# A fused scan, MLP and token-mix kernel: the front's steps in a written list, TensorE in the weight conversions, and token-mix weights moved beside the middle MLP blocks

## The chip, the cores and the metric

One core of a Trainium2 chip runs the whole program. The metric is the device time of one execution in microseconds (us); of a kernel the median of its runs is given. The engines in the rows are PE (TensorE; PEld is its weight load), DVE (VectorE), ACT (ScalarE), POOL (GpSimd) and SP, whose queue starts nearly all DMA transfers.

## The reference, cut to what matters

Three parts follow each other. All inputs are 4 batches of 768 positions.

```python
for t in range(768):                                   # attention: 4 x 8 heads, state 48 x 48
    y[:, :, t] = einsum('bhd,bhde->bhe', q_t, state)
    v_old = einsum('bhde,bhd->bhe', state, k_t)        # k normalised by its length
    state += beta_t * outer(k_t, v_t - v_old)
x = y as (4, 768, 384)
u = x + real(fft(fft(x, axis=1), axis=2))              # MLP part
x = u + relu(layernorm(u) @ w_ch1) @ w_ch2             # 384 -> 1536 -> 384
theta = x @ w_theta                                    # token mix
u = x + w_tok_r @ (x * cos(theta)) + w_tok_i @ (x * sin(theta))
out = u + relu(u @ w_ch)
```

The weights come as 64-bit floats, everything else and the output as 32-bit.

## The kernel before, in words

**Precision and conversions.** A product of two fp32 values is made of three passes in the format fp32r, high by high, high by low and low by high (`mm3`, L71 to L74). So each weight is kept as two fp32r tiles, hi and lo. `Split.steps` (L93 to L123) makes them: one step takes a 128 x 384 piece of 64-bit numbers, loads it with a DMA on SP into a raw tile (L107), takes the absolute value of the high words on ScalarE (L110), puts a 32-bit number together with six VectorE instructions (L111 to L116), and makes hi and lo with three GpSimd ones (L120 to L122). w1 and w2 have 12 such pieces each, 24 conversions in all, that take turns three by three. Their tiles are those of the MLP's residual u (two buffers, the raw tile) and of its transposed input uh, ul (one buffer each, the working tiles named w_...ag).

**Attention.** The sequential recurrence is done in chunks of 64 positions. `gram(w)` (L201) loads keys and queries with two DMAs for each half of a step d and makes their products sm on TensorE; `solve(w)` (L223) turns a triangular system for 32 chunk pairs at once by elimination on VectorE, a loop of 30 steps with one product tmp and one sum T each (L258, L261); there are six solves. `load(d)` brings queries, keys and values; `chunks(d)` prepares the scan (the YU tiles take four copies on VectorE, L309 and L315); `scan(g)` carries the state X over one chunk of all heads: short matmuls pu, ps and py (through the helper at L199), with copies and products of X on ScalarE and GpSimd in between. 24 steps d hold 48 scans, 12 to a batch.

**MLP.** After the twelve scans of a batch its Fourier matmuls follow, then three blocks of 256 positions, twelve in all. `prepare`, `prepare_1` (pm, L530) and `prepare_2` make a block's input; then twelve times an up group ph (`ffn_up`, nine matmuls L72 to L74) and a down group pc (`ffn_down`, six matmuls L595 to L598). Block q + 1 is prepared inside block q, at the places f = 0, 4 and 11 (LEAD). A block's result is stored to the scratch x2scr.

**Token mix.** `TokenMix.weights` converts w_theta and w_tok_r beside the last MLP blocks; `late_weights` converts w_tok_i (12 steps) and w_ch (3) once the MLP's w1 and w2 are used up, and into their tiles. `phases(b)` makes for six tiles of 128 positions theta (pth), its sine and cosine (L846 begins the reduction n) and the products z as hi and lo tiles (L862). `run` then makes for each half hf of the positions the sums over w_tok_r (`real`) and w_tok_i (`imaginary`), in PSUM tiles ty, and the last product with w_ch (`channels`). z tiles lie in a pool of their own for the first six and in w2's tiles for three more. Batch 0 has an order of its own, with the real sums of half 0 and two of half 1 ahead of the late conversions.

**What sets the order.** `attention_steps` is a generator; tables say at which d a solve or a gram is issued (SOLVES, GRAMS, AHEAD). `attend(n)` takes n of its pieces between the groups of the MLP; in the front, each piece is followed by one conversion until the first batch has its twelve scans; then nine conversions more (CONV_PRE), then three for each f of the first block as long as any are left. A scheduler (TCARGS) finally orders each engine's instructions by a simulated timeline, so what stands behind what on an engine is to be seen in the order below.

```python
    while not state["fed"]:
        attend(1)
        if state["chunks"] >= CONV_AT:
            late = late or fr.solve_end
            with tc.issue_after(late.ins):
                next(split, None)
```

Of the kernel before, what the change touches and what calls it, by code (L numbers as in the profile page):

```python
# [33 lines left out]
F64_LEAST = 2.0 ** -15  # L34
F64_MOST = float(np.array([0x47EFFE00], np.uint32).view(np.float32)[0])
# [6 lines left out]
SOLVES = (2, 6, 7, 13, 15)  # L42
GRAMS = (1, 6, 9, 13)
CONV_AT = 0
CONV_PRE = 9
# [3 lines left out]
RPACE = 15  # L49
# [3 lines left out]
AHEAD = {3: (), 4: (5,), 5: (6, 7)}  # L53
FIXD = ()
SUBD = 0
# [21 lines left out]
class Split:  # L77
# [15 lines left out]
    def steps(self, stage, act=False):  # L93

        nc, step = self.nc, self.STEP
        for c, s in self.todo:
# [40 lines left out]
class Front:  # L137
# [19 lines left out]
    def open_attention(self, ctx):  # L157
# [43 lines left out]
    def gram(self, w, c0=0, c1=2 * C):  # L201

        nc, FE, TK, B2 = self.nc, self.FE, self.TK, self.B2
        if c0 == 0:
            self.KQ[w] = self.sol.tile([P, NI, 2 * C], F32, tag="KQ", name=f"KQ{w}", bufs=2)
# [3 lines left out]
        for d in range(4 * w, 4 * w + 4):  # L209
            for h in range(0, 8, step):  # L210
                n = slice(8 * (d % 4) + h, 8 * (d % 4) + h + step)
                kt = self.sol.tile([P, step, 8 * C // step], F32, tag="kt", name=f"kt{d}_{h}_{c0}", bufs=NKT)
                for par in range(2):
                    nc.sync.dma_start(kt[FE[par]], src[par, d, :, h:h + step])
                sm = self.mw([P, step, c1 - c0], f"sm{d}_{h}_{c0}")
                for i in range(step):
                    for par in range(2):
                        k = kt[FE[par], i, :]
                        self.mm(sm[TK[par], i, :], k[:, 0:C], k[:, c0:c1])
                nc.scalar.activation(kq[:, n, c0:c1], sm, AF.Copy)  # L220
                if c0 == 0:
                    for par in range(2):
                        (nc.vector if w in FIXD else nc.gpsimd).tensor_copy(kq[B2[par], n, 0:32], kq[B2[par], n, 32:64])  # L223

    def solve(self, w):
        nc, sol, sml = self.nc, self.sol, self.sml
        T = sol.tile([P, 32, 32], F32, tag="T", name=f"T{w}")
        nc.vector.transpose(T.rearrange("p j i -> p j i"), self.KQ[w][:, :, 0:32].rearrange("p n j -> p j n"))
        diag = T.rearrange("p i j -> p (i j)")[:, 0:1024:33]

        def small(nm, bufs=1):
            return sml.tile([P, 32], F32, tag=nm, name=f"{nm}_{w}", bufs=bufs)
# [54 lines left out]
    def chunks(self, d):  # L287
# [3 lines left out]
        if d % 4 == 0:  # L291
            self.solved(d // 4)
# [736 lines left out]
```

## Time and profile before

| | before |
|---|---|
| three runs | 1001.2, 1001.59, 1005.55 us; median 1001.59 |
| profiled execution | span 1217.0 us, 23437 instructions |
| PE | 1126.0 us busy, 93%, 9312 matmuls (PEld 957.3, 79%) |
| DVE | 682.7 us, 56%, 1574 instructions |
| ACT | 394.8 us, 32%, 982 |
| POOL | 387.5 us, 32%, 504 |
| granted TensorE clock, mean | 0.666 of full speed |
| HBM | 58 GB/s over the span |

The profiled execution is the one that all rows come from, and its span is its own time: 215 us more than the median of the runs without a profile. Busy time is what an engine spent in instructions. The page's slices show two parts: in the first eight of 40 (some 240 us) PE is busy 45 to 76% and DVE mostly over 90%; in all others PE is at 90% or more.

### The profile page before, as it was taken

To read this page: it belongs to the slowest core of one execution; us is meant where nothing else is said; L and a number is where in the kernel's file an instruction comes from. 1 tells how busy PE (TensorE), PEld (TensorE's weight loads), DVE (VectorE), ACT (ScalarE), POOL (GpSimd) and SP (SyncE) were. 2 spreads that over 40 slices of the span, in tenths; PEclk is the share of its full clock that TensorE was granted. 3 is DMA by queue.
4 is the path that set the end of the run, shared out by engine and by line. 5 is a ranking of instruction groups with operands and counts; after the bars stand their busy time and mean duration, and the time that the engine had idled before them with its cause. 6 is when DMAs were issued, how large, how long until landed. Compare 5 with 4: busy or idle time off the path is not lost.

```text
span 1217.0 us, 23437 instructions
## 1 busy us (share of the span) xinstructions
PE 1126.0 (93%) x9312; PEld 957.3 (79%) x9312; DVE 682.7 (56%) x1574; ACT 394.8 (32%) x982; POOL 387.5 (32%) x504
## 2 busy tenths in 40 slices
PE   5675664999999999999999999999999999999998
PEld 4564553778788888788888898888988888888887
DVE  5999999645666632576212464744579732450401
ACT  2243343423332343244352121212545411460300
POOL 5257764341131113024120242430235421350210
PEclk9995555666666666666666666666666666666666
DMA  6223431221030021012030021311132201110000
GB/s 190 70 87 94 121 110 50 79 72 60 29 110 21 28 86 59 27 40 68 27 106 14 26 78 40 91 40 32 47 104 65 85 14 35 38 40 20 20 13 26
DMA packets 42206, 71.87 MB, mean 59 GB/s; under 512 B 6833, under 2 KB 27057, under 8 KB 42097
## 3 DMA queue, kind: packets, MB, share of 16 engines
q1 hardware_dynamic: 41328, 68.02, 18.7%
q0 software_dynamic: 768, 2.36, 0.7%
q8 instruction: 73, 1.20, 0.4%
q14 instruction: 37, 0.30, 0.1%
HBM read 56.20 MB, written 14.16 MB: 58 GB/s over the span
## 4 chain that ended last, share of the span: by engine, by line
PE 83%; DVE 13%; issue 1%; DMA 1%; ACT 1%; POOL 0%; SPq 0%; ACTq 0%; DVEq 0%; POOLq 0%
PE pc L595 6%; PE ph L72 6%; PE ph L74 6%; PE ph L73 6%; PE pc L598 6%; PE pc L596 6%; PE ty L73 6%; PE ty L72 6%; PE ty L74 6%; PE sm L199 3%; PE pm L530 3%; DVE tmp L258 3%; DVE T L261 3%; PE py L199 2%; PE pg L457 2%; PE pu L199 2%
## 5 line engine op out<-in xcount | busy, mean ns | idle before, releaser
L586 DVE SCALAR_TENSOR_TENSOR hl<-ph,hh 128x256 fp32r<-128x256 f32 x144 | 60.1, 421 | 196.6 <-ACT hh L585 164.1
L72 PE MATMUL ph<-uh,w1h 128*128 128x256 f32 x432 | 151.9, 355 | 0.0
L74 PE MATMUL ph<-uh,w1l 128*128 128x256 f32 x432 | 148.5, 345 | 0.0
L73 PE MATMUL ph<-ul,w1h 128*128 128x256 f32 x432 | 148.2, 344 | 0.0
L595 PE MATMUL pc<-w2h,hh 128*128 128x384 f32 x288 | 127.6, 443 | 0.0
L585 ACT ACTIVATE hh<-ph 128x256 fp32r<-128x256 f32 x144 | 54.5, 383 | 208.6 <-PE ph L74 183.0
L596 PE MATMUL pc<-w2l,hh 128*128 128x384 f32 x288 | 121.4, 422 | 0.0
L199 PE MATMUL sm<-kt 48*64 48x128 f32 (+1 forms) x896 | 87.5, 354 | 30.7 <-DMA kt<-in_kq_dram 17.3
L73 PEld LDWEIGHTS ph<-ul,w1h 128*128 128x128 f32 x432 | 100.7, 233 | 6.6 <-issue 2.2
L72 PEld LDWEIGHTS ph<-uh,w1h 128*128 128x128 f32 x432 | 97.4, 226 | 8.3 <-issue 2.5
L74 PEld LDWEIGHTS ph<-uh,w1l 128*128 128x128 f32 x432 | 101.0, 234 | 2.3 <-issue 0.8
L199 PEld LDWEIGHTS sm<-kt 48*64 48x64 f32 x896 | 67.5, 186 | 43.7 <-ACT KQ L220 12.5
L598 PE MATMUL pc<-w2h,hl 128*128 128x384 f32 x288 | 98.2, 425 | 0.0
L261 DVE TENSOR_TENSOR T<-T,tmp 128x30 f32<-128x30 f32 (+9 forms) x180 | 73.1, 406 | 4.2
L258 DVE TENSOR_TENSOR tmp<-T 128x30 f32<-128x30 f32 (+9 forms) x180 | 72.9, 405 | 4.3
L284 POOL TENSOR_SCALAR_AFFINE_SELECT YQ<-KQ 64x512 f32<-64x512 f32 x48 | 33.1, 690 | 131.5 <-PE py L199 122.8
L199 PE MATMUL py<-X,YQ 112*64 112x48 f32 (+1 forms) x768 | 54.4, 259 | 22.3 <-ACT X L340 22.1
L595 PEld LDWEIGHTS pc<-w2h,hh 128*128 128x128 f32 x288 | 63.3, 220 | 8.4 <-issue 4.0
L596 PEld LDWEIGHTS pc<-w2l,hh 128*128 128x128 f32 x288 | 63.2, 220 | 7.2 <-issue 1.7
L199 PE MATMUL pu<-X,YU 128*64 128x48 f32 (+1 forms) x768 | 46.2, 262 | 23.6 <-ACT X L352 11.7
L199 PEld LDWEIGHTS py<-X,YQ 112*64 112x64 f32 (+1 forms) x768 | 45.3, 184 | 28.7 <-ACT X L340 23.9
L199 PEld LDWEIGHTS pu<-X,YU 128*64 128x64 f32 (+1 forms) x768 | 38.7, 181 | 33.9 <-ACT X L352 12.2
(282 smaller groups left out, 2524.6 us busy)
## 6 DMA issues: line engine op xcount, KB each, us to landing
kt<-in_kq_dram SPq DMA_DIRECT2D x96, 96.0 KB, 2.2
w_0raw<-in_w_dram SPq DMA_DIRECT2D x15, 384.0 KB, 3.4
YQ<-in_qt_dram SPq DMA_DIRECT2D x48, 96.0 KB, 2.4
Y<-in_kn_dram SPq DMA_DIRECT2D x48, 96.0 KB, 2.4
X<-in_v_dram SPq DMA_DIRECT2D x48, 96.0 KB, 2.5
ysc<-y SPq DMA_DIRECT2D x24, 192.0 KB, 2.1
x2scr<-u SPq DMA_DIRECT2D x12, 384.0 KB, 2.8
xt<-x2scr SPq DMA_DIRECT2D x24, 192.0 KB, 2.4
```

Source lines behind the costliest of these rows:

```text
L72: nc.tensor.matmul(out, lh, rh, start=start, stop=False)
L73: nc.tensor.matmul(out, lh, rl, start=False, stop=False)
L74: nc.tensor.matmul(out, ll, rh, start=False, stop=stop)
L199: self.nc.tensor.matmul(o, l, r, start=True, stop=True, skip_group_check=True)
L258: nc.vector.tensor_tensor(pr, T[:, j + 1:, j:j + 1].to_broadcast([P, n, j]), T[:, j, 0:j].unsqueeze(1).to_broadcast([P, n, j]), ALU.mult)
L261: nc.vector.tensor_tensor(T[:, j + 1:, 0:j], T[:, j + 1:, 0:j], pr, ALU.add)
L530: nc.tensor.matmul(pm, G[:, ch, j * P:(j + 1) * P], cs2[:, ch, :], start=(ch == 0), stop=(ch == KD - 1))
L585: nc.scalar.activation(hh, ph, AF.Relu)
L586: self.up_end = nc.vector.scalar_tensor_tensor(hl, ph, 0.0, hh, ALU.max, ALU.subtract)
L595: nc.tensor.matmul(self.pc[i], hh[:, i * P:(i + 1) * P], wh, start=(f == 0), stop=False)
L596: nc.tensor.matmul(self.pc[i], hh[:, i * P:(i + 1) * P], wl, start=False, stop=False)
L598: nc.tensor.matmul(self.pc[i], hl[:, i * P:(i + 1) * P], wh, start=False, stop=(f == KF - 1))
```

## The change

- **The front's order.** The tables are replaced by one written list (PLAN): k, q and g are grams of one step d, s a solve, j its transposes, l loads, c chunks, n a scan, w or W conversions, f the Fourier constants, and | an end of a piece. `attend` takes one piece at a time everywhere, and none any more for the last block.
- **Loads of grams.** Keys and queries are padded on the host so that one DMA of 112 rows takes the place of two, and half of the tiles lie in the MLP's pool.
- **Conversions of w1 and w2.** The absolute value is scaled by 2^-80, which takes one VectorE instruction away (L113). The low part is formed in PSUM: three matmuls of 128 x 384 add the 32-bit number by an identity (fp32) and subtract the two parts by a negative identity (fp32r); hi and the PSUM tile are copied on ScalarE. No GpSimd instruction is left. The token mix's conversions keep the GpSimd form, without L113.
- **Copies.** The YU copies of d = 0 to 5 go from VectorE to ScalarE (COPY_ACT), and the small diagonal copies of the first two grams from GpSimd to ScalarE (DIAG_ACT). A solve by two blocks of 16 with a join is written too, and BLOCKED = 0 leaves it off.
- **First block.** Conversions are asked for by number (`converted`); block 1 is prepared at f = 5, 7, 11 (LEAD_0), and all 24 are then done at f = 5.
- **Token mix.** w_tok_i is cut in two halves. The first has a tile pair of its own and is converted in `weights`; the second, in a new pool, and w_ch are the late steps (9 instead of 15). All z tiles lie in w1's and w2's tiles. Batch 0 runs through the same loop as the others, with three late steps (RPACE) after each real sum of half 0.

```diff
-F64_LEAST = 2.0 ** -15
-F64_MOST = float(np.array([0x47EFFE00], np.uint32).view(np.float32)[0])
+F64_SCALE = 2.0 ** -80
+F64_LEAST = 2.0 ** -95
+F64_MOST = float(np.array([0x47EFFE00], np.uint32).view(np.float32)[0]) * F64_SCALE
...
-SOLVES = (2, 6, 7, 13, 15)
-GRAMS = (1, 6, 9, 13)
-CONV_AT = 0
-CONV_PRE = 9
+BLOCKED = 0
+COPY_ACT = (0, 1, 2, 3, 4, 5)
...
-RPACE = 15
+RPACE = 3
...
+PLAN = """k0 k3 k2 k1 q2 w1 g7 q0 l0 q1 q3 f l1 g4 s0 g5 g6 j0 c0 c1 n0 n1 n2 l2 W1 W1 W1 w1
+ W1 n3 c2 l3 c3 W1 W1 W1 g9 W1 W1 w1 n4 g10 W1 n5 s1 j1 l4 g8 W1 W1 g11 c4 n6 n7 W1 n8
+ W1 l5 n9 l6 c5 n10 W1 W1 n11 c6 s2 | l7 c7 j2 n12 n13 n14 n15 g13 g15 l8 c8 g12 g14 l9 c9 s3
+ | | n16 n17 l10 | n18 n19 l11 c10 | c11 g19 | | g17 g18 n20 n21 g16 n22 j3 l12 c12 | n23 l13 |
+ c13 n24 | | n25 l14 s4 n26 c14 n27 l15 c15 | g20 g21 g22 g23 n28 n29 l16 j4 c16 s5 | n30 n31 w1 |
+ l17 c17 n32 n33 | l18 c18 n34 | n35 | l19 c19 n36 j5 | | n37 | l20 n38 n39 l21 c20 c21 | n40 n41
+ l22 c22 n42 | n43 l23 c23 | n44 n45 | | n46 n47"""
...
-    def steps(self, stage, act=False):
+    def steps(self, stage, act=False, sums=None):
 
         nc, step = self.nc, self.STEP
         for c, s in self.todo:
@@ -107,12 +113,21 @@
             nc.sync.dma_start(raw, rows.bitcast(U32))
             raw = raw.rearrange("p (n w) -> p n w", w=2)
             low, high = raw[:, :, 0], raw[:, :, 1]
-            nc.scalar.activation(af, high.bitcast(F32), AF.Abs)
-            nc.vector.tensor_scalar(g, high, 0x80000000, None, ALU.bitwise_and)
+            nc.scalar.activation(af, high.bitcast(F32), AF.Abs, scale=F64_SCALE)
+            nc.vector.tensor_scalar(g, high, 0x80000000, 0x80000000, ALU.bitwise_xor, ALU.bitwise_and)
             nc.vector.tensor_scalar(af, af, F64_LEAST, F64_MOST, ALU.max, ALU.min)
-            nc.vector.tensor_scalar(a, a, 3, 0x40000000, ALU.logical_shift_left, ALU.bitwise_xor)
-            nc.vector.scalar_tensor_tensor(a, a, 0x7FFFFFFF, g, ALU.bitwise_and, ALU.bitwise_or)
+            nc.vector.scalar_tensor_tensor(a, a, 3, g, ALU.logical_shift_left, ALU.bitwise_xor)
             nc.vector.tensor_scalar(g, a, 0xFF800000, None, ALU.bitwise_and)
+            if sums:
+                ps, eye, minus = sums(f"{self.name}_{c}_{s}s")
+                nc.vector.scalar_tensor_tensor(ol, low, -(2.0 ** -52), gf, ALU.mult, ALU.mult)
+                nc.scalar.activation(oh, af, AF.Copy)
+                nc.tensor.matmul(ps, eye, af, start=True, stop=False)
+                nc.tensor.matmul(ps, minus, ol, start=False, stop=False)
+                nc.tensor.matmul(ps, minus, oh, start=False, stop=True)
+                nc.scalar.activation(ol, ps, AF.Copy)
+                yield
+                continue
...
+            nc.sync.dma_start(kt[0:P - 16], src[d, :, h:h + step])
...
+    def copy(self, d, o, i):
+        if d in COPY_ACT:
+            self.nc.scalar.activation(o, i, AF.Copy)
+        else:
+            self.nc.vector.tensor_copy(o, i)
...
-            nc.vector.tensor_copy(yu[B2[par], par, :, 32:64], TT[B2[par], n, :])
+            self.copy(d, yu[B2[par], par, :, 32:64], TT[B2[par], n, :])
...
+    def sums(self, name):
+        return self.psg.tile([P, DM], F32, tag="g", name=name), self.ident, self.eyes
...
+    def convert(self):
+        if (n := next(self.split, None)) is not None:
+            self.done = n[0]
...
+    a, c = fr.w1.steps(fr.stage, 0, fr.sums), fr.w2.steps(fr.stage, 0, fr.sums)
+
+    fr.split = chain.from_iterable(zip(range(k, k + 3), x) for k in range(1, 24, 6) for k, x in ((k, a), (k + 3, c)))
+    fr.done = 0
+
+    def converted(n):
+        while fr.done < n:
+            fr.convert()
...
-    for _ in range(CONV_PRE):
-        next(split, None)
     order = [(q, f) for q in range(len(blocks)) for f in range(KF)]
+    converted(3)
     h = fr.ffn_up(*blocks[0], 0, *ready[0])
     for n, (q, f) in enumerate(order):
         more = q + 1 < len(blocks)
-        for _ in range(3 if q == 0 else 0):
-            next(split, None)
-        if f in LEAD and more:
-            prep(q + 1, LEAD.index(f))
+        lead = LEAD if q else LEAD_0
+        if f in lead and more:
+            if q == 0:
+                converted(24)
+            prep(q + 1, lead.index(f))
         nh = None
         if n + 1 < len(order):
             q1, f1 = order[n + 1]
+            if q1 == 0:
+                converted(6 * (f1 // 3) + 3)
             nh = fr.ffn_up(*blocks[q1], f1, *ready[q1])
+        if q == 0:
+            converted(6 * (f // 3) + 4 + f % 3)
         fr.ffn_down(*blocks[q], f, ready[q][0], *h)
         h = nh
-        if not back or f % 2 == 0 and (q, f) >= SPREAD or q == len(blocks) - 1:
-            attend(PACE)
+        if not back or f % 2 == 0 and (q, f) >= SPREAD:
+            attend(1)
...
+        self.ti = [Split(nc, p, io["wti"][:, 0:S // 2], NT, S // 2, "wti0")]
...
-        self.zp = ctx.enter_context(tc.tile_pool(name="t_z0", bufs=NT, side="left"))
+        p = ctx.enter_context(tc.tile_pool(name="t_wi", bufs=1, side="left"))
+        self.ti.append(Split(tc.nc, p, self.io["wti"][:, S // 2:], NT, S // 2, "wti1"))
...
-        self.ti = Reuse(nc, w1, io["wti"], NT, S, "wti")
         self.ch = Reuse(nc, w2, io["wch"], KD, DM, "wch")
         self.us = [t[:, KF - KD:KF, :] for t in (w2.hi, w2.lo)]
-        self.zs = [t[:, f, :] for f in range(KD, KF - KD) for t in (w2.hi, w2.lo)]
-        ti, ch = (w.steps(self.stage, ACTL) for w in (self.ti, self.ch))
-        return chain(islice(ti, NT), ch, ti)
+        self.zs = [t[:, :, f * P:(f + 1) * P] for f in range(KF) for t in (w1.hi, w1.lo)]
+        self.zs += [t[:, f, :].rearrange("p (e c) -> p e c", c=P) for f in range(KD, KF - KD) for t in (w2.hi, w2.lo)]
+        return chain.from_iterable(w.steps(self.stage, ACTL) for w in (self.ch, self.ti[1]))
...
-            if b == 0:
-                for e in range(KD):
-                    real(0, e)
-                more()
-                for e in range(2):
-                    real(1, e, True)
-                for _ in rest:
-                    pass
-                for _ in range(NZ - NT):
-                    next(nxt)
-                for e in range(KD):
-                    imaginary(0, e)
-                channels(0, True)
-                for e in range(2):
-                    imaginary(1, e)
-                real(1, 2)
-                imaginary(1, 2)
-            else:
-                for hf in range(2):
-                    for e in range(KD + 1):
-                        if e < KD:
-                            real(hf, e)
-                            if hf == 0 and e < NZ - NT:
-                                next(nxt, None)
-                        if e:
-                            imaginary(hf, e - 1)
-                    if hf == 0:
-                        channels(0)
+            for hf in range(2):
+                for e in range(KD + 1):
+                    if e < KD:
+                        real(hf, e)
+                        if hf == 0 and e < NZ - NT:
+                            more()
+                            next(nxt, None)
+                    if e:
+                        imaginary(hf, e - 1)
+                if hf == 0:
+                    channels(0)
```

In the order of the two programs 20 conversions stand ahead of the first up group before, and 19 in the change.

**PE, around the first scans** (pu, py and ps are the scan's matmuls, pw and pt those of chunks, w_1_0s and w_2_0s the PSUM tiles of conversions). Before:

```order
L199 MATMUL pu_725<-X_83,YU_78 64x48 x8
L199 MATMUL pw_700<-YU_79,Y_86 48x64
L199 MATMUL pt_850<-YU_80,A_845 32x32 x6
L199 MATMUL pw_700<-YU_79,Y_86 48x64 x15
L199 MATMUL ps_736<-X_83,Y_85 48x48 x8
L199 MATMUL py_747<-X_83,YQ_81 64x48 x8
L199 MATMUL pt_850<-YU_80,A_845 32x32 x9
```

Changed:

```order
L219 MATMUL pu_711<-X_83,YU_78 64x48 x8
L219 MATMUL pw_689<-YU_79,Y_86 48x64
L125 MATMUL w_1_0s<-w_1_0ag,ident 128x384
L126 MATMUL w_1_0s<-w1l,eyes 128x384
L127 MATMUL w_1_0s<-w1h,eyes 128x384
L219 MATMUL pw_689<-YU_79,Y_86 48x64 x15
L219 MATMUL ps_722<-X_83,Y_85 48x48 x8
L219 MATMUL py_733<-X_83,YQ_81 64x48 x8
L125 MATMUL w_2_0s<-w_2_0ag,ident 128x384
L126 MATMUL w_2_0s<-w1l,eyes 128x384
```

Three matmuls of a conversion now stand between the matmuls of the scan and its chunks, on the same in-order engine.

**PE, in the first MLP block, ahead of the seventh up group** (ph0_0_6 is that group, pc0_0 the block's output, w2_10_0s and w2_11_0s the PSUM tiles of conversions 23 and 24). Before:

```order
L598 MATMUL pc0_0_0_2066<-w2h_94,hl0_0_4_2616 128x384
L598 MATMUL pc0_0_1_2067<-w2h_94,hl0_0_4_2616 128x384
L72 MATMUL ph0_0_6_2894<-uh0_0_1965,w1h_92 128x256
L73 MATMUL ph0_0_6_2894<-ul0_0_1966,w1h_92 128x256
L74 MATMUL ph0_0_6_2894<-uh0_0_1965,w1l_93 128x256
```

Changed:

```order
L125 MATMUL w2_10_0s_3069<-w2_10_0ag_3062,ident_61 128x384
L219 MATMUL pu17_2815<-X0_83,YU2_80 64x48 x8
L126 MATMUL w2_10_0s_3069<-w2l_97,eyes_87 128x384
L127 MATMUL w2_10_0s_3069<-w2h_96,eyes_87 128x384
L219 MATMUL sm14_4_0_2575<-kt14_4_0_2573 64x128 x8
L219 MATMUL py16_2806<-X0_83,YQ0_81 64x48
L219 MATMUL ps17_2826<-X0_83,Y30_85 48x48 x8
L219 MATMUL py16_2806<-X0_83,YQ0_81 64x48 x7
L219 MATMUL pa9_2597<-TN2_2261,KQ2_1109 32x32 x16
L125 MATMUL w2_11_0s_3084<-w2_11_0ag_3077,ident_61 128x384
L78 MATMUL ph0_0_6_3095<-uh0_0_1965,w1h_94 128x256
L79 MATMUL ph0_0_6_3095<-ul0_0_1966,w1h_94 128x256
```

Where the up group followed a down group directly, matmuls of the scan's steps 16 and 17 and of the last conversions now stand ahead of it.

**SP, at the last block's store** (x2scr<-u3_2 is that store; xt0_5 is the last tile of batch 0 that the token mix reads, wti and wch are loads of late conversions). Before:

```order
L831 DMA xt0_4_9215<-x2scr_57 128x384
L107 DMA wti_5_0raw_9549<-in_wti_dram 128x768
L831 DMA xt0_5_9276<-x2scr_57 128x384
L107 DMA wti_2_0raw_9510<-in_wti_dram 128x768
L602 DMA x2scr_57<-u3_2_8612 256x1x384
L831 DMA xt1_0_9717<-x2scr_57 128x384
```

Changed:

```order
L915 DMA xt0_4_9352<-x2scr_57 128x384
L113 DMA wch_2_0raw_9487<-in_wch_dram 128x768
L684 DMA x2scr_57<-u3_2_8579 256x1x384
L113 DMA wti1_4_0raw_9680<-in_wti_dram 128x768
L915 DMA xt1_0_9511<-x2scr_57 128x384
L915 DMA xt1_1_9603<-x2scr_57 128x384
L915 DMA xt1_2_9704<-x2scr_57 128x384
L915 DMA xt1_3_9942<-x2scr_57 128x384
L915 DMA xt0_5_9398<-x2scr_57 128x384
L113 DMA wti1_1_0raw_9567<-in_wti_dram 128x768
```

## Rows read from the trace of the kernel before

**Rows 1.** Windows: us, PE busy (x) PEld DVE ACT POOL, granted PEclk, DMA share, GB/s.

```profile
59.00:140.00 81.00, 50.17 (x767) 43.43 (x768) 78.39 (x164) 29.78 (x74) 57.00 (x59) 0.71 0.31 94
140.00:214.00 74.00, 42.86 (x764) 38.24 (x761) 72.12 (x157) 29.56 (x82) 41.30 (x46) 0.52 0.31 89
0.00:234.00 234.00, 148.49 (x2216) 127.42 (x2217) 209.03 (x458) 83.72 (x208) 125.65 (x170) 0.72 0.34 99
234.00:1217.00 983.00, 977.50 (x7100) 829.91 (x7096) 473.66 (x1117) 311.03 (x775) 261.86 (x334) 0.65 0.17 50
```

**Rows 2.** Waits of PE, total us, times, longest; two from 0:234, one from 234:1217.

```profile
PE py L199 <- ACT X L340: 22.1, 6, 6.5
PE pu L199 <- ACT X L352: 11.7, 3, 7.6
...
PE ty L72 <- ACT zrh L862: 1.4, 1, 1.4
```

**Rows 3.** Windows of tile tmp, one solve each: DVE busy (x), PEclk, DMA share, GB/s.

```profile
0.00:64.00 64.00, 21.83 (x60) 1.00 0.44 124
64.00:140.00 76.00, 33.63 (x60) 0.69 0.33 100
140.00:215.00 75.00, 29.37 (x60) 0.52 0.31 88
```

**Rows 4.** Timeline: start us, us, engine, line, operation; second and third solve.

```profile
94.83 2.50 DVE L258 TENSOR_TENSOR tmp<-T 128x228 f32<-128x228 f32 x1
95.14 0.99 POOL L122 TENSOR_TENSOR w2l<-w_0ag 128x384 fp32r<-128x384 f32 x1
96.09 0.98 POOL L121 TENSOR_TENSOR w_384ag<-w_384ag,w1h 128x384 f32<-128x384 f32 x1
...
198.88 0.40 DVE L258 TENSOR_TENSOR tmp<-T 128x228 f32<-128x228 f32 x1
```

**Rows 5.** Windows of w_768ag, then w_1152ag (DVE, ACT, POOL); lines of the front by form.

```profile
0.00:234.00 234.00, 9.21 (x18) 1.66 (x3) 9.10 (x9) 0.72 0.34 99
...
0.00:234.00 234.00, 5.63 (x15) 1.67 (x3) 7.07 (x6) 0.72 0.34 99
...
L113 DVE TENSOR_SCALAR w_1152ag<-w_1152ag 128x384 uint32<-128x384 uint32 x3 | 1.1, 355 | 0.1
L309 DVE COPY YU<-TT 32x256 f32<-32x256 f32 x22 | 9.0, 407 | 1.5 <-PE pu L199 0.8
L315 DVE COPY YU<-TT 32x256 f32<-32x256 f32 x22 | 7.6, 345 | 0.6
```

**Rows 6.** Windows of lines L120, L121, L122 in the front: POOL busy (L121 with DVE first).

```profile
0.00:234.00 234.00, 24.61 (x20) 0.72 0.34 99
0.00:234.00 234.00, 0.00 (x0) 25.10 (x20) 0.72 0.34 99
0.00:234.00 234.00, 22.68 (x20) 0.72 0.34 99
```

**Rows 7.** DMA issues: queue, operation, count, KB each, median us to landing.

```profile
w_0raw<-in_w_dram SPq DMA_DIRECT2D x15, 384.0 KB, 3.4
xt<-x2scr SPq DMA_DIRECT2D x24, 192.0 KB, 2.4
```

**Rows 8.** Chain that ended last: start us, us; fp32 matmuls count as two, so x2 once.

```profile
218.95 1.06 PE pm L530 x2
...
304.26 0.47 PE pc L598 x2
...
309.99 2.94 PE pm L530 x6
```

**Rows 9.** Timeline of ACT in the token mix: first and last step of one z tile.

```profile
880.43 0.58 ACT L846 ACTIVATE n<-pth,magic 128x384 f32<-128x384 f32 x1
...
890.76 0.53 ACT L862 ACTIVATE zrh<-n 128x384 fp32r<-128x384 f32 x1
```

**Rows 10.** Windows, late in the token mix, all engines as in rows 1.

```profile
1158.40:1161.80 3.40, 3.40 (x12) 3.40 (x12) 0.00 (x0) 0.00 (x0) 0.00 (x0) 0.52 0.00 0
```

More of the change, by code (lines that the diff above doesn't have):

```diff
@@ L48 @@
 NXT = 4
-RPACE = 15
+RPACE = 3
+MIXACT = False
 NMW = 1
@@ L52 @@
 LEAD = (0, 4, 11)
[L53 to L55 removed]
+LEAD_0 = (5, 7, 11)
 LATE = {6: 1}
@@ L176, in init @@
         nc = self.nc
+        s = self.sml.tile([P, 1], F32, name="warm")
+        nc.gpsimd.memset(s, 1.0)
+        nc.scalar.activation(s, s, AF.Sqrt)
         for t in self.YU:
@@ L208, in gram @@
         src = self.io["kt" if c1 == C else "kq"]
-        for d in range(4 * w, 4 * w + 4):
-            for h in range(0, 8, step):
-                n = slice(8 * (d % 4) + h, 8 * (d % 4) + h + step)
+        for h in range(0, 8, step):
+            n = slice(8 * (d % 4) + h, 8 * (d % 4) + h + step)
+            if c1 == C and d % 4 >= NKT:
+                kt = self.up.tile([P, 2, DM], F32, tag=("u", "u", "un")[d % 4 - NKT], name=f"kt{d}_{h}_{c0}",
+                                  **({"bufs": 1} if d % 4 - NKT == 2 else {}))
+                kt = kt.rearrange("p a b -> p (a b)")[:, 0:8 * C].rearrange("p (s c) -> p s c", s=step)
+            else:
@@ L225, in solve @@
+            nc.scalar.activation(kq[:, n, c0:c1], sm, AF.Copy)
+            for par in range(2):
+                nc.gpsimd.tensor_copy(kq[B2[par], n, 0:32], kq[B2[par], n, 32:C])
     def solve(self, w):
         nc, sol, sml = self.nc, self.sol, self.sml
-        T = sol.tile([P, 32, 32], F32, tag="T", name=f"T{w}")
+        nb = 2 if w < BLOCKED else 1
+        m = 32 // nb
+        buf = sol.tile([P, 33 * 32], F32, tag="T", name=f"T{w}")
+        T = buf[:, 0:1024].rearrange("p (i j) -> p i j", j=32)
@@ L235, in solve @@
+        s0, rc, nr, g = (small(nm) for nm in ("s0", "rc", "nr", "g"))
         nT = small("nT", 2)
-        dg = small("dg")
+        dg = ng = small("dg")
         nc.vector.tensor_copy(dg, diag)
-        nc.gpsimd.affine_select(out=T, in_=T, compare_op=ALU.is_gt, fill=0.0, base=0,
-                                pattern=[[1, 32], [-1, 32]], channel_multiplier=0)
+        for b in range(nb):
+            nc.gpsimd.affine_select(out=E[:, b], in_=E[:, b], compare_op=ALU.is_gt, fill=0.0, base=0,
+                                    pattern=[[1, m], [-1, m]], channel_multiplier=0)
@@ L641, in front @@
     fr.init()
-    steps = fr.attention_steps()
-    state = {"chunks": 0, "fed": 0}
+    steps = fr.attention_steps(PLAN)
+    state = {"fed": 0}
+    fr.scans = 0
     back = []
@@ L651, in attend @@
                 return
-            g = state["chunks"]
+            g = fr.scans
             if g // 2 % 6 >= 2 and fr.stage1 < g // NCH - 1:
@@ L658, in attend @@
                 return
-            s = next(steps, None)
-            if s is not None:
-                state["chunks"] = s
+            next(steps, None)
             feed()
@@ L665, in feed @@
         b = state["fed"]
-        if state["chunks"] >= NCH * (b + 1) and fr.stage1 >= b - 1:
+        if fr.scans >= NCH * (b + 1) and fr.stage1 >= b - 1:
             with tc.high_priority(offset=FOFF):
@@ L775, in stage @@
                 raw = st.tile([P, 2 * DM], U32, tag="raw", name=name + "raw")
-                return (raw, *(st.tile([P, DM], U32, tag=n, name=name + n) for n in "ag"))
-            for w in (self.th, self.tr):
-                yield from w.steps(stage)
+                a = st.tile([P, DM], U32, tag="a", name=name + "a")
+                return raw, a, raw.rearrange("p (n w) -> p n w", w=2)[:, :, 1]
+            for w in (self.th, self.tr, *self.ti):
+                yield from w.steps(stage, MIXACT)
     def stage(self, name):
```

191 lines of the change are left out of this document (108 added, 83 removed).

## Prediction

> **What bounds the kernel now.** I read the stretches first, then who waited for whom, then single instructions. The windows split the span at 234 us, where the first MLP matmul starts [rows 1]. After it TensorE is busy 977.5 of 983 us; the longest of its waits behind a named engine there is 1.4 us, for a z tile [rows 2]. Nothing but TensorE work can shorten that stretch. Before it, TensorE is busy 148.5 of 234 us and VectorE 209; between 59 and 214 us VectorE has 150.5 of 155 us. So the front is a VectorE queue, and TensorE waits in it: 22.1 us at py and 11.7 at pu for copies of the scan [rows 2].
>
> Much of those 209 us is not work. The 60 instructions of one solve's elimination take 21.8 us in the first solve, 33.6 in the second and 29.4 in the third [rows 3]. The instruction rows say why: a 228-element product takes 2.50 us when GpSimd runs conversion steps across it, and 0.40 us when GpSimd is quiet [rows 4]. The conversions show the same: 18 VectorE instructions on the 768 columns take 9.21 us (0.51 each), 15 on the 1152 columns 5.63 (0.375 each) [rows 5].
>
> **The change, part by part.** *Conversions of w1 and w2.* Each loses one VectorE instruction (0.35 us clean [rows 5]), and all three GpSimd ones; ScalarE now rounds the high part, and TensorE forms the remainder in PSUM with three 384-column matmuls, which ScalarE copies out. Counted in the order of both programs, 20 conversions stand ahead of the first MLP matmul before and 19 now; three solves and the first batch's Fourier inputs stand there in both.
>
> *VectorE in the front.* Removed: 19 instructions at 0.375 (7.1 us), the twentieth conversion's six (2.3), and 22 of 44 copies into YU, now on ScalarE (22 x 0.376, the mean of its two rows: 8.3) [rows 5]. That makes 17.7. Then the contention: 19.3 us of it stand in the solve loops (33.6 + 29.4 - 2 x 21.8 [rows 3]), about 13 in the conversions (the 0.14 us between the two rows [rows 5], over the 96 of 117 instructions that are not on the 1152 columns), and I put 8 to the small instructions and copies between them: 40. The three conversion lines are 72.4 [rows 6] of GpSimd's 125.7 us [rows 1], and more than that of what really collides, since the rest holds many short copies; I take 28 of the 40, between bounds of 20 and 40. VectorE's work is then 209 - 17.7 - 28 = 163 us. Its 25 idle us (234 - 209) stay. One wait is new: nine conversions follow each other between the second and third solve, through two raw tiles. A tile needs 3.4 us to land [rows 7], an estimated half microsecond of issue, a 0.55 us pass on ScalarE (its two rows of that size [rows 9] are 0.58 and 0.53) and some 2 us of VectorE, 6.5 for two, or 3.3 per conversion against 2 of VectorE: 8 us over seven of them. The first MLP matmul comes at 163 + 25 + 8 = 196 instead of 234: **-38**.
>
> *TensorE in the front.* A conversion's fp32 matmul is priced by pm (128x385, fp32): 1.06 us; the two fp32r ones by pc, 0.24 each at the dense stretch's clock, some 0.3 here: 1.7, and 32 us for 19 [rows 8]. 148.5 + 32 = 181 of 196 us: hidden, but barely, and the scan's matmuls stand behind them in order. ScalarE gains 48 short copies and 38 of 0.55: some 37 us on 84, hidden.
>
> *TensorE after it.* Five conversions instead of four are left, and all now use TensorE: 5 x (0.98 + 0.47) = 7.3 us [rows 8]. The other matmul counts differ by a few small ones, -0.5. **+7**, on the path.
>
> *The first block.* Conversions 20 to 24 have one raw tile (block 0 holds the other), and TensorE's order puts their matmuls ahead of the seventh up group. From the sixth up group on, each of the last two costs about 6.5 us of landing, Abs and VectorE, against some 4.5 us of other TensorE work in between: **+4**, from 0 to 10.
>
> *Token mix.* Half of wti moves beside blocks 7 to 10, where TensorE hides it, and nine late conversions remain instead of fifteen. But the first batch now runs like the others: only half 0's real part stands ahead of what needs the sixth z tile. In the order, 36 matmuls (8.5 us at 0.24) and four transposes (2 us) lie between pth of that tile and its first use; the chain from n to the last z copy took 10.3 us [rows 9]. With two staging steps in the same queues I take **+3**, from 0 to 10. The xt load of that tile stands on SP behind the last block's store, a staging load and four xt loads: about 8 us after the block's end, with 2.4 of landing [rows 7]; TensorE has some 12 us until then, so no term. BLOCKED is 0, so the join code issues nothing.
>
> [...]
>
> **Sum.** The profiled execution: 1217 - 38 + 7 + 4 + 3 = 1193. Its span is 215 us over the median of the runs shown, 1001.6. If the VectorE-bound 234 us are the same there, the dense part is 767.6 of 983, 0.78. The front's gain is not scaled; the added matmuls become 5.5; the two waits, which are not TensorE's, I leave at 8 in all. 1001.6 - 38 + 5.5 + 8 = **977**. With the terms' bounds (-48 to -28, waits of 0 to 20) this case reaches from 959 to 999.
>
> **Rivals.** *TensorE and ScalarE take VectorE's place in the front.* For it: 181 busy us, and the waits for the scan's copies, 22.1 + 11.7 us [rows 2], may not be filled but pushed back, since conversions stand between the scan's steps in order. 148.5 + 32 + 34, and 6 for the start, makes 221: -13, and 1001.6 - 13 + 8 = 997. Against it: the scan ran in 59 to 214 us with 62 us idle beside it.
>
> *All contention goes, and loads keep up.* 209 - 17.7 - 40 + 25 = 176: -58, and with 5.5 and small waits 952. [...]
>
> *Slower: the first block runs in lockstep.* The loads for conversions 21 to 24 stand on SP behind kt, X and ysc transfers that wait for scans and grams, whose matmuls stand on TensorE behind the conversions. If every one of the five makes that round with TensorE idle, a round is 3.9 for the load, 0.55 Abs, 2 VectorE, 0.55 copy, 1.4 matmuls, 8.4 us: 42 instead of 4, and 1001.6 - 38 + 5.5 + 42 + 4 = 1015. It decides from about 30 us of such idle time on. Against it: the change gives TensorE up to six up and down groups, some 17 us, ahead of them.
>
> *The contention is not the conversions'*: GpSimd's X products and selects, which stay, take its place beside VectorE, the front loses only the 17.7, the loads' 8 return, and the waits stand: 1001.6 - 10 + 5.5 + 4 = 1001. Against it: of the GpSimd steps that lie across the 2.50 us, those shown are conversion lines [rows 4].
>
> **Chances.** The forecast 0.60, TensorE in the front 0.14, the larger gain 0.15, the slower first block 0.06, contention that stays 0.05. About 0.5% (5 us) is what a measurement of this kernel can tell from no change: under 996.6 is faster. Of the forecast 0.58 lies there, of the first rival 0.10, all of the second: 0.83. Slower takes the lockstep case and a little of the last: 0.07. The rest is 0.10. The range, 950 to 998, leaves out the lockstep case, the last rival, half of the first and the far end of the second.
>
> **What would show it.** Right: ph starts near 196; the elimination's 60 instructions fall to 22 to 26 us in all three solves; GpSimd is busy some 50 us in the front; TensorE's idle after it is under 15 us in all. Wrong: solve loops still near 30 us, py and pu waits over 35 us in the front, or a hole of over 10 us before the seventh up group or before the sixth z tile's first use.

## The result, and the profile after

| | before | changed |
|---|---|---|
| median of the runs | 1001.88 us (1001.2 to 1005.55, 4 runs) | 977.92 us (975.43 to 979.0, 4 runs) |
| ratio, 95% interval | | 0.9752, 0.9731 to 0.9774 |

The time is 24 us shorter, close to the forecast of 977.0. The forecast's sum holds less well: the front gave less than was forecast, and the rest of the program cost less.

The page of the changed kernel: the span, the busy times, and the slices of PE, DVE, POOL and the granted clock.

```profile
span 977.1 us, 23403 instructions
...
PE 890.2 (91%) x9408; PEld 803.5 (82%) x9408; DVE 634.9 (65%) x1490; ACT 426.4 (44%) x1072; POOL 311.2 (32%) x422
...
PE   5659788699999999999999999999987999999988
...
DVE  4989859956998872699231665888789637263411
...
POOL 2201133323123014124313224654535526144321
PEclk8557879779999999999999999999998999999999
```

The profile that the rows ahead of the prediction come from was taken in an execution with a lower granted clock (0.67 on the mean) than the timed runs (0.93 to 0.98 where it was recorded); so a second profile of the kernel before was taken (the first experiment), and everything below is compared with that one. Its windows: the front up to the first up group, all behind it, the first block, and batch 0 of the token mix (columns as in [rows 1]).

```profile
0.00:232.00 232.00, 146.28 (x2217) 125.87 (x2217) 208.53 (x457) 83.36 (x207) 122.87 (x170) 0.77 0.35 100
232.00:1001.10 769.10, 736.29 (x7098) 680.43 (x7096) 484.95 (x1118) 306.15 (x776) 265.99 (x334) 0.99 0.21 63
...
232.00:277.20 45.20, 42.55 (x450) 36.60 (x449) 27.11 (x67) 16.47 (x46) 23.82 (x36) 1.00 0.34 99
...
743.00:819.80 76.80, 64.83 (x340) 60.96 (x340) 70.07 (x127) 39.92 (x88) 39.55 (x37) 0.93 0.33 98
```

The same four stretches of the changed kernel:

```profile
0.00:206.00 206.00, 148.68 (x2261) 118.46 (x2261) 165.44 (x408) 115.71 (x291) 52.72 (x95) 0.73 0.41 119
206.00:977.10 771.10, 741.54 (x7150) 685.06 (x7148) 469.51 (x1083) 310.67 (x782) 258.46 (x327) 0.99 0.21 64
206.00:260.60 54.60, 53.95 (x721) 46.90 (x719) 35.86 (x100) 27.92 (x73) 11.68 (x19) 0.97 0.27 80
722.40:794.80 72.40, 61.96 (x332) 58.98 (x331) 50.80 (x85) 32.09 (x69) 33.65 (x33) 0.93 0.22 66
```

The whole gain is in the front: 232.0 to 206.0 us. VectorE's work there fell by 43.1 us and its idle time grew by 17.1 (232.0 - 208.53 = 23.5, 206.0 - 165.44 = 40.6). Behind the front TensorE has 5.2 us more work and 3.2 us less idle time. -26.0 + 5.2 - 3.2 is the span's -24.0.

The elimination loops of the three solves (windows of tile tmp: DVE busy), in the kernel before:

```profile
0.00:65.00 65.00, 22.02 (x60) 1.00 0.44 122
65.00:145.00 80.00, 34.50 (x60) 0.73 0.35 102
145.00:220.00 75.00, 27.83 (x60) 0.58 0.28 81
```

and in the changed one, where all three take what the first always took:

```profile
0.00:65.00 65.00, 21.78 (x60) 0.61 0.48 134
65.00:130.00 65.00, 22.30 (x60) 0.73 0.40 123
130.00:206.00 76.00, 23.43 (x60) 0.84 0.34 102
```

What VectorE waits for in the front has changed. The two longest waits before (start us, us, instruction; in brackets the idle time ahead of it and what ended it):

```profile
18.23 1.92 DVE L228 STREAM_TRANSPOSE T<-KQ 128x1024 f32<-128x1024 f32 x1 [5.89 <-POOL KQ L223]
25.00 0.18 DVE L241 TENSOR_SCALAR s<-s 128x32 f32<-128x32 f32 x1 [4.63 <-ACT s L240]
```

and now (total us, times, longest), with three of them one by one:

```profile
DVE w_0ag L117 <- DMA w_0raw<-in_w_dram: 17.7, 3, 9.2
DVE w_768ag L117 <- DMA w_768raw<-in_w_dram: 7.0, 2, 4.5
...
17.83 0.36 DVE L117 TENSOR_SCALAR w_0ag<-w_0raw 128x384 uint32<-128x384 uint32 x1 [9.19 <-DMA w_0raw<-in_w_dram]
125.88 0.36 DVE L117 TENSOR_SCALAR w_768ag<-w_768raw 128x384 uint32<-128x384 uint32 x1 [4.51 <-DMA w_768raw<-in_w_dram]
137.98 0.39 DVE L117 TENSOR_SCALAR w_0ag<-w_0raw 128x384 uint32<-128x384 uint32 x1 [5.70 <-DMA w_0raw<-in_w_dram]
```

It now waits 24.7 us for raw weight tiles. Of these, 9.2 us lie at the program's start, in the place of the 10.5 us that the kernel before waited there for the first solve's inputs: the first solve's loop begins at 29.80 us now and began at 29.91 us before. The other 15.5 us are new (1.6 us before), and 12.7 of them lie between the loops of the second and the third solve.

### The profile page after: what moved, and what is told of

The parts are those of the page before. It is cut to its first block, busy times and chain, and to the rows that moved or that the text cites. A ratio compares the mean times of both kernels' runs of the same rounds, so it can differ in the third digit from the quotient of the medians.

```text
span 977.1 us, 23403 instructions
## 1 busy us (share of the span) xinstructions
PE 890.2 (91%) x9408; PEld 803.5 (82%) x9408; DVE 634.9 (65%) x1490; ACT 426.4 (44%) x1072; POOL 311.2 (32%) x422
## 4 chain that ended last, share of the span: by engine, by line
PE 59%; DVE 25%; DMA 5%; issue 4%; ACT 4%; POOL 3%; SPq 0%; DVEq 0%; ACTq 0%; POOLq 0%
PE ph L78 4%; PE ph L79 4%; PE pc L677 4%; PE ty L80 4%; PE ty L78 4%; PE ty L79 4%; PE ph L80 4%; PE pc L678 4%; PE pc L680 3%; DVE tmp L302 3%; DVE T L305 3%; PE sm L219 3%; PE pu L219 2%; PE py L219 2%; PE pm L612 2%
## 5 line engine op out<-in xcount | busy, mean ns | idle before, releaser
L78 PE MATMUL ph<-uh,w1h 128*128 128x256 f32 x432 | 126.4, 296 | 1.3 <-DVE ul L656 1.3
L79 PE MATMUL ph<-ul,w1h 128*128 128x256 f32 x432 | 124.4, 289 | 2.3 <-DVE ul L656 2.2
L80 PE MATMUL ph<-uh,w1l 128*128 128x256 f32 x432 | 123.1, 286 | 0.0
L677 PE MATMUL pc<-w2h,hh 128*128 128x384 f32 x288 | 103.5, 359 | 2.7 <-ACT hh L667 2.7
L678 PE MATMUL pc<-w2l,hh 128*128 128x384 f32 x288 | 97.9, 340 | 0.0
L80 PEld LDWEIGHTS ph<-uh,w1l 128*128 128x128 f32 x432 | 83.2, 193 | 0.4 <-issue 0.2
L680 PE MATMUL pc<-w2h,hl 128*128 128x384 f32 x288 | 75.6, 342 | 0.4 <-DVE hl L668 0.3
L378 POOL TENSOR_TENSOR X<-X,nT 64x384 f32<-64x384 f32 x48 | 43.7, 910 | 71.6 <-DMA X<-in_v_dram 55.1
L980 POOL TENSOR_TENSOR w2l<-xT,w2h 128x384 fp32r<-128x384 f32 x24 | 24.7, 1033 | 87.5 <-ACT w2h L979 87.5
L680 PEld LDWEIGHTS pc<-w2h,hl 128*128 128x128 f32 x288 | 49.7, 188 | 2.2 <-DVE hl L668 1.8
```

Of the source, the lines that this page charges most:

```text
L78: nc.tensor.matmul(out, lh, rh, start=start, stop=False)
L79: nc.tensor.matmul(out, lh, rl, start=False, stop=False)
L80: nc.tensor.matmul(out, ll, rh, start=False, stop=stop)
L378: nc.gpsimd.tensor_tensor(x[TK[par], par], x[TK[par], par], nT[TK[par], n].unsqueeze(2).to_broadcast([C, 8, D]), ALU.mult)
L677: nc.tensor.matmul(self.pc[i], hh[:, i * P:(i + 1) * P], wh, start=(f == 0), stop=False)
L678: nc.tensor.matmul(self.pc[i], hh[:, i * P:(i + 1) * P], wl, start=False, stop=False)
```

## The experiments

### The kernel before, profiled again

No edit.

> The kernel before, unchanged, for a second profile. The forecast's working took the front's 234 us as what it also is in the timed runs, and scaled the rest to 767.6 us. If that holds, a profile whose clock is near 0.93 has its first up group (ph) near 234 us and a span near 1000. Rival: the front of the first profile was stretched by its clock too, and ph starts at 215 to 225, so that most of the gain measured in the change lies elsewhere.

The front is 232.0 us and the rest 769.1, in the windows above; one run took 1003.88 us. The forecast had taken 234 and 767.6. So the basis of its sum was right, though the first profile showed 983 us for the rest. Its reading that nothing but TensorE work can shorten the rest was not: at this clock, 0.99 behind the front, TensorE is idle for 32.8 of the 769.1 us, where the first profile has 5.5 of 983.

### Conversions, copies and order apart

Three kernels. The first is the kernel before with the new `steps` (and `eyes` and `sums`):

```diff
-    a, c = fr.w1.steps(fr.stage, SUBD), fr.w2.steps(fr.stage, SUBD)
+    a, c = fr.w1.steps(fr.stage, 0, fr.sums), fr.w2.steps(fr.stage, 0, fr.sums)
```

> The kernel before with the conversions alone in their new form (no GpSimd step, three matmuls, one VectorE step less); order tables, copies and token mix as before. Theory that contention with GpSimd was the price: the second and third solve loops fall to 22 to 25 us, the front by 25 to 35 us, TensorE after it gains 4 to 6, and the time is 970 to 982. Rival, the written order is what pays: within 5 us of 1002.

The second is the changed kernel with the GpSimd form in their place (the VectorE instruction that the change takes away stays away):

```diff
-    a, c = fr.w1.steps(fr.stage, 0, fr.sums), fr.w2.steps(fr.stage, 0, fr.sums)
+    a, c = fr.w1.steps(fr.stage, 0), fr.w2.steps(fr.stage, 0)
```

> The changed kernel with its conversions of w1 and w2 back on GpSimd (the VectorE step stays removed). Contention theory: the solve loops go back to 29 to 33 us, the front grows by 20 to 30 us, TensorE loses 5, and the time is 995 to 1005. Rival, the order pays: 973 to 983.

The third takes the YU copies alone back to VectorE:

```diff
-COPY_ACT = (0, 1, 2, 3, 4, 5)
+COPY_ACT = ()
```

> The changed kernel with all YU copies on VectorE again. The forecast credited the move with 8.3 us of VectorE work in the front: 982 to 987 if the front is still a VectorE queue. Rival, that loads and TensorE now set the front: 976 to 980.

And the last adds the copies on ScalarE to the first:

```diff
-            nc.vector.tensor_copy(yu[B2[par], par, :, 32:64], TT[B2[par], n, :])
+            self.copy(d, yu[B2[par], par, :, 32:64], TT[B2[par], n, :])
...
-            nc.vector.tensor_copy(yu[B1[par], par, :, 0:32], TT[B1[par], n, :])
+            self.copy(d, yu[B1[par], par, :, 0:32], TT[B1[par], n, :])
```

> The kernel before with the new conversions and with the YU copies of d = 0 to 5 on ScalarE; order tables, first block, loads and token mix as before. The new conversions alone gave 993.6, the changed kernel without the copies' move 992.6, the whole change 978. If conversions and copies are the gain and the written order adds nothing of its own, 976 to 982. If the order is what lets the freed VectorE time be used (in the old order the front stayed at 233 us with VectorE idle for 48 of them), 988 to 995.

"Order" is all else that the change does: list, loads, small diagonal copies, first block, token mix.

| conversions | copies | order | median us | ratio to before, interval |
|---|---|---|---|---|
| old | VectorE | old | 1001.9 | 1 |
| new | VectorE | old | 993.6 | 0.9906, 0.9888 to 0.9924 |
| new | ScalarE | old | 989.1 | 0.9882, 0.9856 to 0.9908 |
| new | VectorE | new | 992.6 | 0.9908, 0.9886 to 0.9930 |
| old | ScalarE | new | 996.6 | 0.9948, 0.9929 to 0.9967 |
| new | ScalarE | new | 977.9 | 0.9752, 0.9731 to 0.9774 |

The expectation for the first (970 to 982) was missed, and its rival too. The second came out at the time that contention has (995 to 1005). Of its loops the second solve's takes 30.1 us; the third solve's takes 23.9, where 29 to 33 were expected, and begins at 168.3 us, behind GpSimd's last conversion step (162.9). In the last, the order is what lets the freed time be used (988 to 995). Added one after the other, new conversions give 8.3 us, the copies 4.5 and the order 11.2. What a part gives depends on the others: the order gives 1.0 without the copies and 11.2 with them, and new conversions give 18.7 where copies and order are already changed (996.6 - 977.9). The copies alone and the order alone were not run. The solve loops do what the theory of contention says: in the old order with new conversions they take 22.2 and 22.8 us. But VectorE then stands idle. The front of that kernel, and of the one with the copies:

```profile
0.00:232.90 232.90, 168.52 (x2503) 134.30 (x2503) 185.13 (x459) 116.09 (x278) 70.47 (x130) 0.75 0.40 116
```

```profile
0.00:226.80 226.80, 166.23 (x2503) 133.81 (x2503) 175.43 (x435) 124.33 (x302) 70.58 (x129) 0.76 0.41 119
```

VectorE's work falls from 208.5 to 185.1 and 175.4 us, its idle time rises from 23.5 to 47.8 and 51.4. But the front's length alone doesn't compare: in these two all 24 conversions stand ahead of the first up group (before 20, changed 19), since the scheduler brought the last ones forward, though the tables are those of before. What compares is the end of the first block, where every kernel has all 24 behind it. These two to there:

```profile
0.00:270.10 270.10, 205.72 (x2898) 167.74 (x2899) 216.18 (x550) 127.17 (x309) 74.91 (x135) 0.78 0.35 102
```

```profile
0.00:264.00 264.00, 203.43 (x2898) 167.33 (x2899) 205.69 (x526) 135.43 (x333) 75.10 (x135) 0.79 0.36 104
```

Before it is 277.2 us (232.0 + 45.2), in the changed kernel 260.6 (206.0 + 54.6). So up to there conversions give 7.1 us, copies 6.1 and the order 3.4; what follows takes 723.9, 721.7, 721.1 and, with the order, 716.5. What VectorE waits for in the second of them:

```profile
DVE w_0ag L115 <- DMA w_0raw<-in_w_dram: 13.5, 6, 4.2
DVE w_0ag L115 <- PE w_384s L123: 9.4, 1, 9.4
DVE T L243 <- POOL KQ L238: 6.9, 2, 6.0
DVE s L256 <- ACT s L255: 6.3, 1, 6.3
```

The two waits at a solve's start, 13.2 us, are still there, and 12.3 of them lie ahead of the first solve; in the new order they are 0.7 us in all. But there VectorE waits 9.2 us for its first raw tile instead: the first solve's loop begins at 32.5 us in this kernel and at 29.8 in the changed one, so that the order pays some 2.7 us at this place. The wait of 9.4 us for a conversion's TensorE step is not there in the changed kernel either. Which part of the order pays the rest was not taken apart.

The copies are worth more in the new order (14.7 us) than the 8.3 of work that the forecast gave them, and less in the old one (4.5). Without them the first block shows it (front and first block of that kernel, new order):

```profile
0.00:210.60 210.60, 149.94 (x2293) 119.65 (x2293) 169.90 (x430) 107.42 (x269) 57.64 (x96) 0.73 0.39 117
210.60:282.80 72.20, 67.36 (x901) 56.27 (x901) 49.88 (x136) 34.50 (x89) 12.87 (x23) 0.91 0.23 70
```

The front is only 4.6 us longer than in the changed kernel's profile, but the first block takes 72.2 us instead of 54.6, with more attention matmuls in it (x901 for x721) and 4.8 us of idle TensorE. Of that, some is work that later blocks then lack; why the rest is lost stays open.

### GpSimd's load put back without its waits

Behind each of the first 19 conversions GpSimd works on a tile that nobody reads:

```diff
                 nc.scalar.activation(ol, ps, AF.Copy)
+                if (d := self.dummy(s, c)) is not None:
+                    e = oh[:, 0:2 * P].bitcast(F32)
+                    nc.gpsimd.tensor_scalar(d, e, 1.0, 0.0, ALU.mult, ALU.add)
+                    for _ in range(3):
+                        nc.gpsimd.tensor_tensor(d, e, e, ALU.add)
```

> The changed kernel, and behind each of its first 19 conversions four GpSimd instructions (128 x 256) that read the finished high part and write a tile that nobody reads: GpSimd's load comes back, and no engine waits for it except GpSimd's own later steps. Contention theory: VectorE's busy time before the first up group grows by 15 to 25 us and the second and third solve loops go to 26 to 32 us; the time is 988 to 997. Rival, that the GpSimd steps cost through the waits on their results: VectorE's busy time grows by under 5, and the time is within 3 us of 978.

995.82 us, ratio 0.9927 (0.9898 to 0.9956): 17.9 us lost. The front of this kernel, and the loops of its second and third solve:

```profile
0.00:223.50 223.50, 157.70 (x2260) 125.12 (x2260) 183.81 (x408) 116.19 (x291) 102.23 (x171) 0.69 0.37 110
...
65.00:130.00 65.00, 27.34 (x60) 0.66 0.32 97
130.00:206.00 76.00, 28.68 (x60) 0.76 0.34 103
```

VectorE executes the same 408 instructions in 183.81 us instead of 165.44. One of them, in the timeline (start us, us):

```profile
104.02 2.24 POOL L133 TENSOR_TENSOR dummy<-w2h 128x256 fp32r<-128x256 f32 x3
...
104.99 0.80 DVE L307 TENSOR_TENSOR tmp<-T 128x228 f32<-128x228 f32 x1
```

The same product takes 0.39 us in the changed kernel's second solve:

```profile
82.90 0.39 DVE L302 TENSOR_TENSOR tmp<-T 128x228 f32<-128x228 f32 x1
```

No result of these steps is read. They do delay GpSimd's own later steps, and TensorE is seen waiting for that:

```profile
PE pu L224 <- POOL dummy L133: 3.5, 2, 2.8
```

But VectorE's idle time in the front did not grow (39.7 us, 40.6 in the changed kernel); its busy time did. That settles contention: 18.4 us of VectorE time come back with 49.5 us of GpSimd time (102.23 - 52.72), and the product with 0.80 for 0.39 us is one instance. By what means the one engine slows the other is not shown.

### The token mix of before on the changed front

`TokenMix`, RPACE and the last block's `attend` are taken from the kernel before:

```diff
-RPACE = 3
+RPACE = 15
...
-        if not back or f % 2 == 0 and (q, f) >= SPREAD:
-            attend(1)
+        if not back or f % 2 == 0 and (q, f) >= SPREAD or q == len(blocks) - 1:
+            attend(2 if q == len(blocks) - 1 else 1)
```

> The changed kernel's front with the token mix of before (15 steps beside the MLP, 15 late, z tiles in their own pool, the special order of batch 0, two pieces per group in the last block). The forecast has the new token mix cost 3 us, so this gives 973 to 977. Rival, that the new token mix earns part of the gain: 985 or more.

979.17 us, ratio 0.9775 (0.9748 to 0.9802): no difference from the change that these runs tell, and below the rival's 985. The part that the title names last neither pays nor costs.

### VectorE's wait for raw tiles

First the key and query loads leave SP's queue:

```diff
-            nc.sync.dma_start(kt[0:P - 16], src[d, :, h:h + step])
+            nc.scalar.dma_start(kt[0:P - 16], src[d, :, h:h + step])
```

> The changed kernel with the key and query loads (kt) issued from ScalarE's queue, where they stand behind the copy that frees their tile, instead of SP's, where loads of raw weight tiles stand behind them. If the 25 us that VectorE waited for raw tiles come from that queue, they fall by 8 us or more and the time is 966 to 973. Rival, the raw tiles themselves are too few, or ScalarE's issue costs as much: within 4 us of 978, or slower.

992.07 us, ratio 0.9891 (0.9861 to 0.9922): slower by 14. VectorE's wait for raw tiles is 20.3 us, which is no fall that can be told: in three other kernels with the changed kernel's front (the one above, and two under the next heading) it is 18.7 to 22.0. Other waits came (VectorE, then TensorE, in the front), and why stays open:

```profile
DVE w_0ag L117 <- DMA w_0raw<-in_w_dram: 15.8, 4, 8.1
DVE u L618 <- PE pm L612: 10.5, 1, 10.5
...
DVE w_768ag L117 <- DMA w_768raw<-in_w_dram: 4.5, 1, 4.5
...
PE pu L219 <- ACT X L431: 14.3, 1, 14.3
```

Then a third raw tile, the buffer of un:

```diff
-        raw = self.up.tile([P, 2, DM], F32, tag="u", name=name + "raw")
+        k = self.staged % 3
+        raw = self.up.tile([P, 2, DM], F32, tag=("u", "un", "u")[k], name=name + "raw", **({"bufs": 1} if k == 1 else {}))
         self.staged += 1
```

> The changed kernel with a third raw tile for the conversions of w1 and w2: every third raw tile is the buffer of the normalised MLP input (un), which is idle in the front. If two raw tiles are what makes VectorE wait some 25 us for raw tiles there, that falls by 10 us or more and the time is 965 to 973. Rival, the loads wait in SP's queue behind key and query loads, or the working tiles hold them up: 974 to 981.

982.48 us, ratio 0.9791 (0.9770 to 0.9811): not faster, rather slower, and above both ranges. The wait is 17.5 us, of which 9.4 lie at the program's start; the other 8.1 are fewer than the changed kernel's 15.5 and the 10.7 to 12.9 of the three others, but a second kernel with the third tile (the next heading) has 11.2 again, so that little of the fall is sure. The front stayed at 205.3 us, and these stand in it now:

```profile
DVE w_0ag L117 <- DMA w_0raw<-in_w_dram: 16.8, 5, 9.4
DVE u L619 <- PE pm L613: 7.9, 1, 7.9
...
DVE w_768ag L117 <- DMA w_768raw<-in_w_dram: 0.7, 1, 0.7
...
PE sm L219 <- ACT YU L401: 20.6, 1, 20.6
```

With the third tile VectorE waits at the end of the front for pm, the first block's Fourier matmul, and TensorE waits 20.6 us behind a ScalarE copy into YU, for the scan. So raw tiles are no longer what sets the front alone; the scan's chain through TensorE and ScalarE, the forecast's first rival, lies right behind them.

### Late conversions

```diff
-LATE = {6: 1}
+LATE = {1: 1, 3: 1, 5: 1, 7: 1}
...
-        return chain.from_iterable(w.steps(self.stage, ACTL) for w in (self.ch, self.ti[1]))
+        return chain.from_iterable(w.steps(self.stage, ACTL) for w in (self.ti[1], self.ch))
```

> The changed kernel with four late conversions (of the second half of w_tok_i, now ahead of w_ch) beside the last MLP block instead of one. If the some 10 us of idle TensorE at 725 to 760 come from VectorE's late conversions, the time is 970 to 975. Rival, VectorE is late in the last block already and the idle time only moves: within 3 us of 978.

976.06 us, ratio 0.9752 (0.9721 to 0.9783): the same as the change. The last block and batch 0 of the token mix in it:

```profile
685.10:721.30 36.20, 31.28 (x208) 29.63 (x209) 28.13 (x54) 18.81 (x43) 14.95 (x16) 1.00 0.21 61
721.30:792.20 70.90, 61.24 (x329) 58.06 (x328) 44.56 (x80) 29.86 (x64) 31.31 (x31) 0.93 0.20 65
```

TensorE's idle time in the last block is 4.9 us, in batch 0 9.7, 10.4 in the changed kernel: little moved. With the third raw tile:

> The third raw tile and four late conversions beside the last block together: the effect of the third raw tile with 2 us more, if both stand on their own.

979.38 us, 0.9775 (0.9754 to 0.9797). And with a VectorE step on GpSimd:

```diff
-ACTL = 2
+ACTL = 1
```

> The changed kernel with one VectorE step of each late conversion (the subtraction) on GpSimd instead. VectorE is 90 to 95% busy around the first token-mix sums, where TensorE is idle for some 10 us; nine steps of about 0.5 us leave VectorE. If its work sets that idle time, 972 to 976. Rival, what GpSimd takes over it slows VectorE by as much: 976 to 981.

981.55 us, 0.9784 (0.9763 to 0.9804): no gain; TensorE's idle time in batch 0 is not shorter (74.5 us long with 63.44 busy). None of the variants beats the change clearly.

## Why the prediction was right, and where its sum was not

| term | forecast | measured, second profile of before against the change |
|---|---|---|
| VectorE's work in the front | -46 (209 to 163) | -43.1 |
| its idle time there | +8 | +17.1 (three other kernels with this front: +11.5 to +13.4) |
| first up group | 196, -38 | 206.0, -26.0 (the three: 200.7 to 201.9) |
| TensorE's work behind it | +5.5 | +5.2 |
| idle TensorE, first block | +4 | 2.7 to 0.6 |
| idle TensorE, token mix's batch 0 | +3 | 12.0 to 10.4 |

*Contention* was the right mechanism and nearly the right size. The unread GpSimd steps cost 18.4 us of VectorE time for 49.5 of GpSimd's; by that rate, an estimate, the 72.4 us of conversion lines [rows 6] are worth 26.9, where the forecast took 28. What it did not see is that the program needs the copies and the new order to use all of it: alone the conversions gave 8.3 us of the 24.

*The loads* were the term of the front that was sized too small. The new waits came where the forecast put them, for raw tiles and mostly between the second and the third solve, and the old idle time stayed, as it had it: the 9.2 us at the start took the place of 10.5. But the new waiting at raw tiles measured 15.5 us, and 10.7 to 12.9 in three other kernels with the same front, where 8 were forecast; the half microsecond in it for a load's issue is 0.35 us in the trace of before (SP, w_0raw, median of 15). The three had their first up group at 200.7 to 201.9 us, so that 7 to 12 us of the forecast's 38 were too much. That two raw tiles are the cause, as the forecast has it, is not shown: with a third one it was 8.1 and 11.2 us.

*TensorE in the front* was forecast to gain 32 us of work, and gained 2.4. The matmuls of its 19 conversions do take 29 us there (each counted from the end of the one before), but the scan's became shorter. In the kernel before, then in the changed one (lines of the front: busy, mean ns, idle before):

```profile
L199 PE MATMUL py<-X,YQ 128*64 128x48 f32 (+1 forms) x256 | 22.0, 295 | 24.4 <-ACT X L340 24.2
L199 PE MATMUL pu<-X,YU 112*64 112x48 f32 (+1 forms) x256 | 18.4, 295 | 20.4 <-ACT X L352 9.4 <-issue 4.7 <-POOL X L299 4.5
```

```profile
L219 PE MATMUL py<-X,YQ 112*64 112x48 f32 (+1 forms) x256 | 16.8, 242 | 2.5 <-ACT X L419 2.5
...
L219 PE MATMUL pu<-X,YU 112*64 112x48 f32 (+1 forms) x256 | 13.1, 243 | 0.9 <-POOL YQ L365 0.4 <-issue 0.4
```

The waits of 22.1 and 11.7 us [rows 2] that the first rival pushed back are nearly gone. With the old conversions in the new order they are still 10.6 and 17.3 us, with the new conversions in the old order 7.9 at py and under 4 at pu: it is mostly the conversions that end them.

*The first block* kept TensorE busy 53.95 of 54.60 us: the last five conversions found attention matmuls to hide behind, and neither the +4 nor the rival's lockstep came. *The token mix* cost nothing either, as the old one on the new front shows. So two errors of opposite sign met: the front gave 12 us too little (7 to 8 in the other profiles), and the two waits, +8 by the forecast against -3.2 of idle time measured, were 11 too dear. That the sum lies within 1 us of the time is luck to this extent.

Of the signs that the forecast named, the solve loops (21.8 to 23.4 us) and GpSimd in the front (52.7 us) came. TensorE's idle time behind the front did not: it is 29.6 us, not under 15. The forecast read that stretch from the first profile, with 5.5 us idle; at the clock of the timed runs the kernel before has 32.8.

## What to carry to other kernels

Before taking work from a crowded engine, look at which neighbour stretches its instructions: here some 25 of the 43 us that VectorE gained (43.1 less the 17.7 of steps removed) were no work removed, but the same instructions at the speed they have when GpSimd is quiet. Then ask what the freed engine meets next: the same edit was worth 8 us in the old program and 19 in the one where copies and order had been made for it. And a transfer that was hidden under a slow engine can become a wait when that engine gets faster: here 15.5 us of waits for raw tiles were new, where the kernel before had 1.6 in its front. Adding a buffer took a few us of that wait away at most here, and no time, since the next chain stood right behind it.

## What the runs showed of the hardware

The first profile of before had a granted clock of 0.65 in the long dense stretch [rows 1], the second 0.99, at 983 and 769 us. The time grew by 1.28, less than the clock's ratio of 1.52. The 0.65 is no mean over long stretches of higher and lower clocks, since windows of 10 us at 300, 600 and 1000 us of the first profile show 0.65 each; late in the token mix, 3.4 us in which TensorE is busy throughout have 0.52 [rows 10]. No run here shows why. An unread GpSimd load lengthened the program by 17.9 us, almost exactly the 18.4 us that it added to VectorE's busy time in the front.
